# S4D with a gated unit: exponential as squares, angles without a reciprocal, low parts and skip weights on other engines

## The chip, the cores and the metric

The kernel runs on one core of a Trainium2 chip, as a single launch. The metric is device time in microseconds (us), the median of several runs. Engines are PE (TensorE; its weight load is PEld), DVE (VectorE), ACT (ScalarE), POOL (GpSimd) and SP (which only issues transfers). L705 is line 705 of the kernel before; in the kernel after most lines stand two to four further down (L442 there is L438 here).

## What is computed

`out = x + S4D(xn) + GLU(xn)` with `xn` the layer norm of x, for 2048 tokens, D = 448 channels, N = 256 states and F = 1792 hidden units in fp32. Of the reference this is the core:

```python
dt = exp(log_dt);  A = -exp(log_A_real) + 1j * A_imag;  C = (C_real + 1j * C_imag) * dt
K = 2 * einsum("dn,dnl->dl", C, exp(A * dt * l)).real      # l = 0 .. 2047
y = irfft(rfft(xn, 2L) * rfft(K, 2L))[:L] + xn * D_skip
glu = (sigmoid(xn @ w_gate) * (xn @ w_up)) @ w_down
```

So for every channel and state the kernel needs an exponential (the decay), the magnitude and angle of C, and from these the phases at all lags. The skip term is a weight at lag 0 of K: the kernel adds D_skip there.

## The kernel before

Two generators, `conv()` for the S4D branch and `glu()` for the gated unit, are run in turns (L1117 to L1127): the one with the smaller share of its planned work goes next. What they emit goes through a scheduler that fixes each engine's order of instructions. All products are done as fp32r matmuls with a split of each operand in a high and a low part (xh, xl; wh, wl; hh, hl; dh, dl), three products each.

`glu()` works on groups of up to three blocks of 128 hidden units and on halves of 512 tokens. For each block and half, `gate` issues 22 matmuls of 512 columns into two PSUM tiles gu (L705), a tanh th on ACT (L713), the product hf on DVE (L716), its high part hh on ACT (L721) and low part hl on DVE (L723). Then the down product po (L818, 448 columns, nine matmuls for a piece of 128 tokens in a group of three blocks, so 72 for the eight pieces) is added into acc by DVE (L823). The four PSUM slots of gu serve po, too. The weights of a block come in through one buffer (wraw); ACT casts the high part wh (L755), DVE subtracts for the low one wl (L759).

`conv()` starts with the norm and the transposes of x (L212; the parts xh, xl, xr at L221 to L225). Then comes the prep, in two halves of tiles of 112 x 512 (two groups of 112 channels, 256 states each), interleaved step by step:

- `exp()` (L303 to L318) computes the exponential of the decay logarithm: a rounding on ACT, the rest by a two-part log 2 on DVE, a polynomial of six steps on DVE (L316), an exponent built as an integer (L317), and the last product ex (L318). hdt, four multiples of dt, are made from its last columns on ACT (L354).
- Tanh and Exp of the decay times dt (L360 to L365) give what the powers need; their product pl goes through `turn` (L431): PE transposes (L438) into the PSUM tiles ko and kp, ACT copies (L440).
- The angle of C: the larger of the two absolute values, its reciprocal in four pieces of 128 columns (`pieces`, L320 to L322), the ratio of smaller to larger w, arctangent (L375), signs and offsets (L371 to L391), sine and cosine (L386, L387). L375 and L386 need different function tables.
- The phases U, V, T (L409 to L416) are split in a high part (a cast on ACT, L401) and a low part (a subtraction on POOL, L406); both go to DRAM over SP's queue.

Between the steps of the prep, `x_spec` (L283) sends the first transform of x through PE (L281) into the PSUM tiles tr, ko and kp, from where ACT copies it (L294 for tr, L296 for ko and kp) and stores it. ko, kp and tr have one buffer each; who writes them next waits for the copies.

`kgen` then makes K in 56 chunks: POOL multiplies up magnitudes me, mf for two chunks at a time (L504, L516), ACT squares a part (L529) and makes sines S (L544 to L547) of phases that PE spreads (tr, L538); DVE multiplies them to Et and Ft (L598 to L600; Ft has one buffer), and PE adds products of these in the PSUM tile ko (L612). After each fourth chunk (14 times, a bank) a small matmul (L622) adds the skip weights dm at lag 0, ACT copies ko to ks (L625), and `first_stage` (L562) takes ks to the first step of the transform. The spectra and the inverse follow (L900, L927).

Of the kernel before, what the change touches and what calls it, by code (L numbers as in the profile page):

```python
# [21 lines left out]
N = 256  # L22
# [4 lines left out]
TWO_PI = 2.0 * math.pi  # L27
MAGIC = 1.5 * 2.0**23
# [10 lines left out]
CP = D // 4  # L39
# [91 lines left out]
def s4d_glu_kernel(ctx, tc, io):  # L131
    nc = tc.nc
    hp = tc.high_priority
    v = nc.vector
# [16 lines left out]
    const = ctx.enter_context(tc.tile_pool(name="const", bufs=1, side="left"))  # L151
    ident = const.tile([128, 128], F32, name="ident")
# [16 lines left out]

    lim = const.tile([128, 2, 3], F32, name="lim")  # L170
# [132 lines left out]
    def exp(ex, ki, fr, pl):  # L303

        v.tensor_scalar(ex, ex, lim[:CP, 0, 1:2], lim[:CP, 0, 2:3], ALU.min, ALU.max)
        yield
        nc.scalar.activation(ki, ex, AF.Identity, scale=1.0 / math.log(2.0))
        yield
        ln2h = 0.693359375
        ln2l = math.log(2.0) - ln2h  # L310
        v.scalar_tensor_tensor(fr, ki, -ln2h, ex, ALU.mult, ALU.add)
        v.scalar_tensor_tensor(fr, ki, -ln2l, fr, ALU.mult, ALU.add)
        cs = [1.0 / math.factorial(i) for i in range(8)]
        nc.scalar.activation(pl, fr, AF.Identity, scale=cs[7])
        for i in range(6, 0, -1):
            v.scalar_tensor_tensor(pl, pl, cs[i], fr, ALU.add, ALU.mult)  # L316
        v.tensor_scalar(ki, ki, 127.0, 8388608.0, ALU.add, ALU.mult)  # L317
        v.scalar_tensor_tensor(ex, pl, 1.0, ki.bitcast(F32), ALU.add, ALU.mult)  # L318

    def pieces(t):  # L320
        for i in range(0, 2 * N, 128):
            v.reciprocal(t[:, i : i + 128], t[:, i : i + 128])  # L322

# [17 lines left out]
    def prep(pool, h, srcs):  # L341
# [3 lines left out]
        a3, b3, m3, w3, s3 = (new(n) for n in ("a3", "b3", "m3", "w3", "s3"))  # L345
# [6 lines left out]
        yield from exp(ex, ki, fr, pl)  # L352
# [14 lines left out]
        v.scalar_tensor_tensor(m3, a3, 1e-37, b3, ALU.max, ALU.max)  # L367
        pieces(m3)
        v.tensor_tensor(w3, a3, b3, ALU.min)
        v.tensor_tensor(w3, w3, m3, ALU.mult)  # L370
        v.tensor_tensor(s3, a3, b3, ALU.subtract)  # L371
        nc.scalar.activation(s3, s3, AF.Sign)
        nc.scalar.activation(cr, cr, AF.Sign)
        with tc.issue_after(exps[0].ins):
            nc.scalar.activation(w3, w3, AF.Arctan)  # L375
# [9 lines left out]
        v.scalar_tensor_tensor(w3, w3, -math.pi / 4, s3, ALU.add, ALU.mult)  # L385
# [3 lines left out]
        nc.scalar.activation(w3, w3, AF.Identity, bias=hpi[:CP])  # L389
        v.tensor_scalar(ci, ci, 0.0, -2.0 / TWO_PI, ALU.is_lt, ALU.mult)  # L390
        v.scalar_tensor_tensor(w3, ci, 1.0 / TWO_PI, w3, ALU.add, ALU.mult)  # L391
        yield
# [64 lines left out]
    def kgen(pk):  # L457
# [124 lines left out]
        for g in range(NCK // NCH):  # L582
            for c in range(NCH):
# [36 lines left out]
                if cn % 4 == 3:  # L620
                    ks = tl["ks"]
                    nc.tensor.matmul(  # L622
                        ko[:, :, 0], ident, dm[:, cn // 4], start=False, stop=True, skip_group_check=True
                    )
                    nc.scalar.copy(ks, ko)  # L625
                yield WK / 2
# [391 lines left out]
    def conv():  # L1018
        with tc.tile_pool(name="psk", bufs=1, space=PSUM) as ps_, tc.tile_pool(
# [9 lines left out]
            with tc.tile_pool(name="pst", bufs=1, side="right", reuse_waits="tile") as pst:  # L1029
# [125 lines left out]
```

## Time and profile before

| what | value |
|---|---|
| median of 3 runs | 723.75 us (722.47, 728.36, 723.75) |
| profiled execution | 724.73 us |
| its span, first to last instruction | 722.9 us |
| mean granted clock of PE | 0.980 of full speed |
| PE busy | 676.9 us, 94% of the span |
| DVE busy | 553.6 us, 77% |
| ACT busy | 428.6 us, 59% |
| POOL busy | 361.9 us, 50% |
| chain that ended last | 63% of it on PE, 11% DVE, 9% ACT |

A line of the timeline has the start, the duration, the engine and line, the operation, the written tile and the read ones, and in brackets the idle time ahead of it with what ended it. A line of waits has engine, tile and line that waited, what it waited for, the sum in us, the number of times and the longest. Successive instructions on an engine overlap by some tenths of a us, so what one costs is the distance from start to start where the engine is full. PE's granted clock is given as a share of full speed.

### The profile page before, as it was taken

What the parts mean: (1) busy time and instruction counts of PE and PEld (TensorE: products, weight loads), DVE (VectorE), ACT (ScalarE), POOL (GpSimd) and SP (SyncE); (2) the same over time, 40 slices, a digit from 0 to 9 for tenths busy, and PEclk for the clock granted to TensorE, in tenths of its full rate; (3) what the DMA queues carried; (4) which work ended last, traced back from release to release, by engine and by line L of the source; (5) the groups of instructions that cost most, each with busy time, mean ns of one, the idle gap of its engine ahead of it and who ended that gap; (6) DMA issues with size and microseconds to landing.
All of it is one profiled execution on the core that took longest, in us unless ns stands there. A gap on an engine that the chain in (4) does not pass through costs nothing.

```text
span 722.9 us, 19254 instructions
## 1 busy us (share of the span) xinstructions
PE 676.9 (94%) x7780; PEld 532.5 (74%) x7780; DVE 553.6 (77%) x760; ACT 428.6 (59%) x678; POOL 361.9 (50%) x423
## 2 busy tenths in 40 slices
PE   3898999999999898999999999998999999999995
PEld 2676887778877785666778877877877777776784
DVE  6899887689889899688488988978956555575543
ACT  3655966488688768795686786787642322313320
POOL 2101177656997966775365697586944002441001
PEclk9998999999999999899999999999999999999998
DMA  9948164464254444556942332332269999999845
GB/s 215 240 123 228 39 201 159 149 198 139 63 167 136 136 114 135 151 162 185 261 133 83 106 111 75 96 114 84 61 183 270 267 255 241 252 258 216 200 121 161
DMA packets 102985, 117.25 MB, mean 162 GB/s; under 512 B 13232, under 2 KB 90864, under 8 KB 102896
## 3 DMA queue, kind: packets, MB, share of 16 engines
q1 hardware_dynamic: 78736, 91.87, 46.0%
q10 hardware_dynamic: 21584, 18.24, 9.5%
q0 software_dynamic: 2576, 5.90, 3.0%
q8 instruction: 62, 1.02, 0.6%
q14 instruction: 27, 0.22, 0.1%
HBM read 72.13 MB, written 43.84 MB: 160 GB/s over the span
## 4 chain that ended last, share of the span: by engine, by line
PE 63%; DVE 11%; ACT 9%; DMA 6%; issue 4%; SPq 2%; POOL 2%; ACTq 1%; POOLq 0%; DVEq 0%
PE gu L705 27%; PE po L818 14%; PE sp L900 7%; PE ko L612 5%; PE pv L927 4%; PE tr L538 3%; DVE Ft L600 2%; DVE Et L599 2%; DVE Et L598 2%; ACT S L547 1%; ACT S L545 1%; ACT S L544 1%; SPq L640 1%; DVE pm L452 1%; DMA ph<-ph_d 1%
## 5 line engine op out<-in xcount | busy, mean ns | idle before, releaser
L516 POOL TENSOR_TENSOR me<-me,pm 128x32 f32<-128x32 f32 (+1 forms) x168 | 138.2, 823 | 104.4 <-DVE Et L599 87.9
L516 POOL TENSOR_TENSOR mf<-mf,pm 128x64 f32<-128x64 f32 (+1 forms) x112 | 121.1, 1081 | 4.7
L705 PE MATMUL gu<-xh,wh 128*128 128x512 f32 x336 | 100.8, 407 | 0.9 <-ACT xh L221 0.7
L705 PE MATMUL gu<-xh,wl 128*128 128x512 f32 x336 | 97.3, 397 | 0.0
L705 PE MATMUL gu<-xl,wh 128*128 128x512 f32 x336 | 97.3, 396 | 0.0
L598 DVE TENSOR_TENSOR Et<-me,S 128x1024 f32<-128x1024 f32 x56 | 82.8, 1479 | 11.9 <-ACT S L547 11.8
L818 PE MATMUL po<-dh,hh 128*128 128x448 f32 x224 | 85.5, 382 | 4.3 <-DVE hf L716 2.9
L599 DVE TENSOR_TENSOR Et<-me,S 128x1024 f32<-128x1024 f32 x56 | 78.1, 1394 | 13.3 <-ACT me L529 6.3
L818 PE MATMUL po<-dl,hh 128*128 128x448 f32 x224 | 83.5, 373 | 0.0
L600 DVE TENSOR_TENSOR Ft<-mf,S 128x1024 f32<-128x1024 f32 x56 | 78.7, 1405 | 5.6 <-ACT S L547 2.7
L544 ACT ACTIVATE S<-tr 128x1024 f32<-128x1024 f32 x56 | 57.8, 1032 | 41.9 <-PE tr L538 41.2
L818 PE MATMUL po<-dh,hl 128*128 128x448 f32 x224 | 82.5, 371 | 0.1
L705 PEld LDWEIGHTS gu<-xh,wh 128*128 128x128 f32 x336 | 61.8, 191 | 21.9 <-issue 4.4
L612 PEld LDWEIGHTS ko<-Et,Ft 128*32 128x32 f32 x3584 | 53.8, 110 | 32.4 <-DVE Ft L600 13.7
L612 PE MATMUL ko<-Et,Ft 128*32 128x64 f32 x3584 | 64.6, 221 | 11.9 <-DVE Ft L600 11.4
L705 PEld LDWEIGHTS gu<-xh,wl 128*128 128x128 f32 x336 | 64.3, 192 | 14.9 <-DVE hf L716 0.7
L705 PEld LDWEIGHTS gu<-xl,wh 128*128 128x128 f32 x336 | 64.3, 192 | 13.8
L721 ACT CAST hh<-hf 128x512 fp32r<-128x512 f32 x56 | 35.0, 625 | 65.9 <-DVE hf L716 60.1
L716 DVE SCALAR_TENSOR_TENSOR hf<-th,gu 128x512 f32<-128x512 f32 x56 | 38.2, 682 | 36.9 <-PE gu L705 31.7
L547 ACT ACTIVATE S<-S,hpi 128x1024 f32<-128x1024 f32 x56 | 65.6, 1171 | 1.3 <-issue 1.3
L823 DVE SCALAR_TENSOR_TENSOR acc<-po,acc 128x448 f32<-128x448 f32 x80 | 48.0, 616 | 23.5 <-PE po L818 23.5
L723 DVE TENSOR_TENSOR hl<-hf,hh 128x512 fp32r<-128x512 f32 x56 | 47.7, 851 | 18.2 <-ACT hh L721 18.2
(209 smaller groups left out, 1281.4 us busy)
## 6 DMA issues: line engine op xcount, KB each, us to landing
sk_d<-sk ACTq DMA_DIRECT2D x14, 512.0 KB
sx<-x_d SPq DMA_DIRECT2D x32, 224.0 KB
skl<-sk_d SPq DMA_DIRECT2D x16, 448.0 KB
vp<-v_d SPq DMA_DIRECT2D x16, 448.0 KB
v_d<-vt SPq DMA_DIRECT2D x62, 112.0 KB
ph<-ph_d SPq DMA_DIRECT2D x224, 24.0 KB
wt_d<-wh SPq DMA_DIRECT2D x9, 512.0 KB
wt_d<-wl SPq DMA_DIRECT2D x9, 512.0 KB
```

Of the source, the lines that this page charges most:

```text
L516: ins = nc.gpsimd.tensor_tensor(m[:, :, w + a : 2 * w : n], m[:, :, a:w:n], par(base + i).unsqueeze(2).to_broadcast([128, 4 * DC, w // n]) ...
L544: nc.scalar.activation(rows(cs), pv, AF.Abs)
L547: sins[:] = [nc.scalar.activation(cs, cs, AF.Sin, scale=-TWO_PI, bias=hpi)]
L598: v.tensor_tensor(Et[:, :, :, 32:64], two(me[:, :, 32:64]), S[:, 1::-1], ALU.mult)
L599: v.tensor_tensor(Et[:, :, :, 0:32], two(me[:, :, 0:32]), S[:, 1:3, :, ::-1], ALU.mult)
L600: fts[:] = [v.tensor_tensor(Ft, two(mf), S[:, 3:5], ALU.mult)]
L612: mm = nc.tensor.matmul(ko[32 * j : 32 * j + 32, sl], Ft[:, cc, DC * h + 4 * q + j], Et[:, cc, DC * h + 4 * q + j], start=(k == 0), stop=( ...
L705: glu_mm[:] = [nc.tensor.matmul(ps, a_, b_, start=(n == 0), stop=(n == len(mm) - 1))]
L723: v.tensor_tensor(hl, hf, hh, ALU.subtract)
L818: glu_mm[:] = [nc.tensor.matmul(po, a_[:, bs], w_, start=(n == 0), stop=(n == 3 * fc - 1))]
L823: v.scalar_tensor_tensor(acc[:, b], po, 0.5, acc[:, b], ALU.mult, ALU.add)
L900: mm = nc.tensor.matmul(to, tb[:kk, t, 64 * c : 64 * c + 64], rhs, start=True, stop=True, skip_group_check=True,)
```

## The change

- `exp()`: the polynomial of six steps becomes a product of three factors, with two squares: ACT makes Square(fr + a), Square(s fr + b) and adds a constant to the second; DVE makes (fr + r) fr, (pl + k) sq and their product. The exponent's integer is made by an Identity on ACT instead of L317. Per half DVE has four instructions less there, ACT three more.
- The angle: no reciprocal. The argument of the arctangent is (a - b) / (a + b); the inverse of the sum m starts from an integer operation on its bits (an Identity on ACT that reads and writes int32), and is refined by two steps in which DVE multiplies and ACT squares. Per half that takes the place of four reciprocals, a minimum and a product on DVE and of one Sign on ACT. The offsets of the angle are merged: ACT scales the sign of cr and makes the sign of ci, and DVE's comparison on ci (L390) and a product by s3 go.
- `low()`: the subtraction of the low phase parts goes from POOL to DVE (six instructions).
- The skip weights: the matmul at L622 goes; ACT copies ko to ks, then POOL adds dm into the column of lag 0 of ks.
- Seven constants are set in a tile bz by POOL at the start. The tile m3 becomes two columns wider and is used by `exp()` as well.

In the orders that the scheduler makes of it, these places are the ones that matter below. A name is a tile, with a number of its buffer; `out<-in`.

PE, at the end of the first group's po. In before both transposes of the first half stand behind the last po, here po_825, and ahead of the next gate, gu_849:

```order
L818 MATMUL po_825<-dh_421,hl_509 128x448
L818 MATMUL po_825<-dh_615,hh_667 128x448
L818 MATMUL po_825<-dl_618,hh_667 128x448
L818 MATMUL po_825<-dh_615,hl_668 128x448
L438 MATMUL ko_784<-ident_67,pl_384 128x112 x2
L438 MATMUL kp_788<-ident_67,pl_384 128x112 x2
L705 MATMUL gu_849<-xh_94,wh_836 128x512 x3
```

In after they stand after the sixth of the eight pieces, po_783, with po_818 and po_829 behind them:

```order
L820 MATMUL po_783<-dh_621,hh_673 128x448
L820 MATMUL po_783<-dl_624,hh_673 128x448
L820 MATMUL po_783<-dh_621,hl_674 128x448
L442 MATMUL ko_794<-ident_67,pl_392 128x112 x2
L442 MATMUL kp_798<-ident_67,pl_392 128x112 x2
L820 MATMUL po_818<-dh_265,hh_465 128x448
L820 MATMUL po_818<-dl_266,hh_465 128x448
L820 MATMUL po_818<-dh_265,hl_466 128x448
```

The transposes moved ahead by 18 matmuls.

ACT, at the last group of x_spec's copies (to x1ab), which free ko and kp. In before they stand ahead of the first hdt and of all Tanh and Exp:

```order
L713 ACTIVATE th_663<-gu_621 128x512
L294 COPY x1ab_376<-tr_671 128x896
L296 COPY x1ab_376<-ko_672 128x448
L300 DMA x1_d_59<-x1ab_376 64x2x448
L755 CAST wh_975<-wraw_976 128x1024
L296 COPY x1ab_376<-kp_673 128x448
L300 DMA x1_d_59<-x1ab_376 64x2x448
L354 ACTIVATE hdt_385<-ex_150 112x2 x4
```

In after the first hdt stands 55 rows ahead of the copy from ko, and the sines with their tables are ahead of the copies, too:

```order
L392 ACT_TABLE_LOAD
L392 ACTIVATE m3_389<-w3_387,qpi_75 112x512
L393 ACTIVATE s3_388<-w3_387,qpi_75 112x512
L414 ACTIVATE ki_402<-aim_159 112x512
L405 CAST p01_383<-aim_159 112x512
L297 COPY x1ab_384<-tr_677 128x896
L384 ACT_TABLE_LOAD
L384 ACTIVATE junk_81<-w3_399 112x1
L392 ACTIVATE m3_401<-w3_399,qpi_75 112x512
L393 ACTIVATE s3_400<-w3_399,qpi_75 112x512
L299 COPY x1ab_384<-ko_678 128x448
L299 COPY x1ab_384<-kp_679 128x448
```

Nearly all of the prep's work on ACT moved ahead of the last copies of x_spec.

DVE, ahead of a product hf of the first group (hf_609 in before):

```order
L322 RECIPROCAL m3_379<-m3_379 112x128 x2
L322 RECIPROCAL m3_391<-m3_391 112x128 x3
L759 TENSOR_TENSOR wl_844<-wraw_837,wh_836 128x1024
L322 RECIPROCAL m3_391<-m3_391 112x128
L316 SCALAR_TENSOR_TENSOR pl_384<-pl_384,fr_383 112x514
L316 SCALAR_TENSOR_TENSOR pl_396<-pl_396,fr_395 112x514
L260 SCALAR_TENSOR_TENSOR z_87<-z_87,ve_86 128x8
L716 SCALAR_TENSOR_TENSOR hf_609<-th_607,gu_595 128x512
```

The same product in after (hf_615):

```order
L761 TENSOR_TENSOR wl_848<-wraw_841,wh_840 128x1024
L373 SCALAR_TENSOR_TENSOR w3_387<-m3_389,w3_387 112x512
L372 TENSOR_TENSOR m3_401<-m3_401,w3_399 112x512
L373 SCALAR_TENSOR_TENSOR w3_399<-m3_401,w3_399 112x512
L387 SCALAR_TENSOR_TENSOR pl_404<-pl_404,ki_402 112x512
L718 SCALAR_TENSOR_TENSOR hf_615<-th_613,gu_601 128x512
```

The reciprocals and the last steps of the polynomial are gone from ahead of it, and products of the new angle stand there.

The diff, cut to its core:

```diff
+    bz = const.tile([128, 7], F32, name="bz")
...
-    def exp(ex, ki, fr, pl):
+    def exp(ex, ki, fr, pl, sq):
...
-        cs = [1.0 / math.factorial(i) for i in range(8)]
-        nc.scalar.activation(pl, fr, AF.Identity, scale=cs[7])
-        for i in range(6, 0, -1):
-            v.scalar_tensor_tensor(pl, pl, cs[i], fr, ALU.add, ALU.mult)
-        v.tensor_scalar(ki, ki, 127.0, 8388608.0, ALU.add, ALU.mult)
+        nc.scalar.activation(ki, ki, AF.Identity, scale=8388608.0, bias=bz[:CP, 3:4])
+        nc.scalar.activation(pl, fr, AF.Square, bias=bz[:CP, 0:1])
+        nc.scalar.activation(sq, fr, AF.Square, scale=EXP_S, bias=bz[:CP, 1:2])
+        nc.scalar.activation(sq, sq, AF.Identity, bias=bz[:CP, 2:3])
+        v.scalar_tensor_tensor(ex, fr, EXP_R, fr, ALU.add, ALU.mult)
+        v.scalar_tensor_tensor(pl, pl, EXP_K, sq, ALU.add, ALU.mult)
+        v.tensor_tensor(pl, pl, ex, ALU.mult)
         v.scalar_tensor_tensor(ex, pl, 1.0, ki.bitcast(F32), ALU.add, ALU.mult)
...
-        v.scalar_tensor_tensor(m3, a3, 1e-37, b3, ALU.max, ALU.max)
-        pieces(m3)
-        v.tensor_tensor(w3, a3, b3, ALU.min)
-        v.tensor_tensor(w3, w3, m3, ALU.mult)
+        v.scalar_tensor_tensor(m3, a3, 1e-37, b3, ALU.max, ALU.add)
+        nc.scalar.activation(w3.bitcast(I32), m3.bitcast(I32), AF.Identity, scale=-1.0, bias=bz[:CP, 4:5])
         v.tensor_tensor(s3, a3, b3, ALU.subtract)
-        nc.scalar.activation(s3, s3, AF.Sign)
+        v.tensor_tensor(m3, m3, w3, ALU.mult)
+        v.scalar_tensor_tensor(w3, m3, -2.0, w3, ALU.add, ALU.mult)
+        nc.scalar.activation(m3, m3, AF.Square, scale=-1.0, bias=one[:CP])
+        nc.scalar.activation(m3, m3, AF.Square, bias=bz[:CP, 5:6])
+        v.scalar_tensor_tensor(w3, m3, 0.75, w3, ALU.add, ALU.mult)
+        v.tensor_tensor(w3, w3, s3, ALU.mult)
         nc.scalar.activation(cr, cr, AF.Sign)
+        nc.scalar.activation(cr, cr, AF.Identity, scale=1.0 / TWO_PI)
+        nc.scalar.activation(ci, ci, AF.Sign, bias=bz[:CP, 6:7])
         with tc.issue_after(exps[0].ins):
             nc.scalar.activation(w3, w3, AF.Arctan)
...
-        v.scalar_tensor_tensor(w3, w3, -math.pi / 4, s3, ALU.add, ALU.mult)
         nc.scalar.activation(m3, w3, AF.Sin, bias=qpi[:CP])
         nc.scalar.activation(s3, w3, AF.Sin, scale=-1.0, bias=qpi[:CP])
         v.scalar_tensor_tensor(w3, w3, -math.pi / 4, cr, ALU.add, ALU.mult)
-        nc.scalar.activation(w3, w3, AF.Identity, bias=hpi[:CP])
-        v.tensor_scalar(ci, ci, 0.0, -2.0 / TWO_PI, ALU.is_lt, ALU.mult)
-        v.scalar_tensor_tensor(w3, ci, 1.0 / TWO_PI, w3, ALU.add, ALU.mult)
+        v.scalar_tensor_tensor(w3, w3, 0.25, ci, ALU.add, ALU.mult)
...
-            nc.gpsimd.tensor_tensor(lo, src, slots[f"P{i}"][:, h], ALU.subtract)
+            v.tensor_tensor(lo, src, slots[f"P{i}"][:, h], ALU.subtract)
...
-                    nc.tensor.matmul(
-                        ko[:, :, 0], ident, dm[:, cn // 4], start=False, stop=True, skip_group_check=True
-                    )
                     nc.scalar.copy(ks, ko)
+                    nc.gpsimd.tensor_tensor(ks[:, :, 0], ks[:, :, 0], dm[:, cn // 4], ALU.add)
...
+                for i, c in enumerate((EXP_A, EXP_B, EXP_C, 127.0 * 8388608.0, float(0x7EF30000), 0.5, 1e-37)):
+                    nc.gpsimd.memset(bz[:, i : i + 1], c)
```

More of the change, by code (lines that the diff above doesn't have):

```diff
@@ L27 @@
 TWO_PI = 2.0 * math.pi
+EXP_A, EXP_B, EXP_C = -0.8713653843588568, 0.07851670935535562, 0.011531916857233048
+EXP_K, EXP_S, EXP_R = 15.06237810040421, 0.03720672317048426, 3.5715240100230314
 MAGIC = 1.5 * 2.0**23
@@ L312, in exp @@
         v.scalar_tensor_tensor(fr, ki, -ln2l, fr, ALU.mult, ALU.add)
-        cs = [1.0 / math.factorial(i) for i in range(8)]
-        nc.scalar.activation(pl, fr, AF.Identity, scale=cs[7])
-        for i in range(6, 0, -1):
-            v.scalar_tensor_tensor(pl, pl, cs[i], fr, ALU.add, ALU.mult)
-        v.tensor_scalar(ki, ki, 127.0, 8388608.0, ALU.add, ALU.mult)
+        nc.scalar.activation(ki, ki, AF.Identity, scale=8388608.0, bias=bz[:CP, 3:4])
[5 more added lines that the diff above has]
+        v.tensor_tensor(pl, pl, ex, ALU.mult)
         v.scalar_tensor_tensor(ex, pl, 1.0, ki.bitcast(F32), ALU.add, ALU.mult)
-    def pieces(t):
-        for i in range(0, 2 * N, 128):
-            v.reciprocal(t[:, i : i + 128], t[:, i : i + 128])
     SF = [CP, 2 * N]
@@ L344, in prep @@
         new = lambda n, sh=SF, dt=F32: pool.tile(sh, dt, name=n, bufs=2)
-        a3, b3, m3, w3, s3 = (new(n) for n in ("a3", "b3", "m3", "w3", "s3"))
+        a3, b3, w3, s3 = (new(n) for n in ("a3", "b3", "w3", "s3"))
+        sq = new("m3", [CP, 2 * N + 2])
+        m3 = sq[:, : 2 * N]
         ki, fr, pl = new("ki", [CP, 2 * N + 2], I32), new("fr", [CP, 2 * N + 2]), new("pl", [CP, 2 * N + 2])
@@ L351, in prep @@
         nc.scalar.activation(b3, ci, AF.Abs, scale=lim[:CP, 1, 0:1])
-        yield from exp(ex, ki, fr, pl)
+        yield from exp(ex, ki, fr, pl, sq)
         for i, c in enumerate((0.5, -1.0, 1.0 / TWO_PI, 2.0)):
```

## Prediction

> **What bounds the kernel now.** I read first the page (busy times, chain), then the waits of TensorE, then the windows between 30 and 100 us, then the timelines of the engine that each wait names.
>
> The page's busy line of PE and its chain by engine, then, from the list of waits, what PE stood idle for (us in total, times, longest):
>
> ```profile
> PE 676.9 (94%) x7780; PEld 532.5 (74%) x7780; DVE 553.6 (77%) x760; ACT 428.6 (59%) x678; POOL 361.9 (50%) x423
> ...
> PE 63%; DVE 11%; ACT 9%; DMA 6%; issue 4%; SPq 2%; POOL 2%; ACTq 1%; POOLq 0%; DVEq 0%
> ```
>
> ```profile
> PE tr L212 <- DVE xn L270: 12.1, 1, 12.1
> PE ko L612 <- DVE Ft L600: 11.4, 10, 2.3
> PE po L818 <- DVE hf L716: 2.9, 1, 2.9
> PE gu L705 <- DVE xr L225: 2.7, 1, 2.7
> PE po L818 <- ACT hh L721: 1.4, 1, 1.4
> ```
>
> PE is the bound: 46 us of the 722.9 are not PE work, 12.1 of them before the first transpose, which the change does not touch. So an edit gains only if it shortens PE's work, closes one of these gaps, or spares the half clock that a gap brings. The prep of the convolution, where nearly all of the change lies, runs from 30 to 105 us. There the 2.9 us gap stands (PE's timeline, then the windows' row of these ten us: busy times, granted clock behind POOL's, DMA):
>
> ```profile
> 57.24 0.84 PE L705 MATMUL gu<-xl,wh 128*128 128x512 f32 x3
> ...
> 59.96 0.47 PE L818 MATMUL po<-dh,hl 128*128 128x448 f32 x1
> 63.35 0.74 PE L818 MATMUL po<-dh,hh 128*128 128x448 f32 x1 [2.91 <-DVE hf L716]
> ...
> 69.11 0.38 PE L818 MATMUL po<-dh,hl 128*128 128x448 f32 x1
> ```
>
> ```profile
> 60.00:70.00 10.00, 7.09 (x26) 6.08 (x22) 9.57 (x18) 4.84 (x12) 0.20 (x1) 0.66 0.74 208
> 70.00:80.00 10.00, 10.00 (x53) 9.14 (x51) 7.88 (x18) 9.95 (x22) 0.00 (x0) 1.00 0.39 98
> ```
>
> The gate's matmuls are done at 58, but the product that the next po needs comes off VectorE at 63.3. Behind the gap the granted clock is low: 0.66 over ten us is 6.8 us at a half, and 15 po take 5.76 us from 63.35 to 69.11, where 0.20 each at full clock (the step of the rows around 75.81 below, 18 po in 3.65) gives 3.05. The gap costs 2.9 and its half clock 2.7 more. VectorE was late for this reason:
>
> ```profile
> 55.35 4.19 DVE L322 RECIPROCAL m<-m 112x128 f32<-112x128 f32 x5
> ...
> 60.53 0.94 DVE L322 RECIPROCAL m<-m 112x128 f32<-112x128 f32 x1
> 61.39 1.23 DVE L316 SCALAR_TENSOR_TENSOR pl<-pl,fr 112x514 f32<-112x514 f32 x2
> ...
> 62.61 0.68 DVE L716 SCALAR_TENSOR_TENSOR hf<-th,gu 128x512 f32<-128x512 f32 x1
> ```
>
> Reciprocals (0.84 each) and polynomial steps (0.6) stood ahead of hf. ScalarE, in turn, is full from 70 to 80 (9.95 of 10 us) already.
>
> **The change part by part.** VectorE first. Per half the exponential loses six steps of 0.6 and one of 0.33 and gets three of 0.6; the angles lose four reciprocals of 0.84, one of 0.33 and get one of 0.6 more. That is 2.1 and 3.1 us, 10.4 over both halves; the six low parts put 6 x 0.6 = 3.6 back. hf is then no longer behind eight reciprocals (6.7 us), it comes at about 59, and the gap at 60 closes: -2.9 and -2.7.
>
> ScalarE gets twelve instructions more, six per half (7.3 us at 0.61), and a fourth table load (1.28) where there were three. Its durations, from its timeline (start to start, since they overlap):
>
> ```profile
> 64.34 0.90 ACT L294 COPY x1ab<-tr 128x896 f32<-128x896 f32 x1
> 65.13 0.55 ACT L296 COPY x1ab<-ko 128x448 f32<-128x448 f32 x1
> ...
> 67.23 1.05 ACT L755 CAST wh<-wraw 128x1024 fp32r<-128x1024 f32 x1 [1.55 <-DMA wraw<-in_B_w_up_dram]
> ...
> 70.58 0.60 ACT L721 CAST hh<-hf 128x512 fp32r<-128x512 f32 x1
> 71.09 0.51 ACT L360 ACTIVATE ki<-ex,hdt 112x256 f32<-112x256 f32 x1
> 71.51 0.47 ACT L354 ACTIVATE hdt<-ex 112x2 f32<-112x2 f32 x4
> 71.88 0.71 ACT L364 ACTIVATE pl<-fr,one 112x512 f32<-112x512 f32 x1
> 72.49 0.71 ACT L365 ACTIVATE ki<-ki,one 112x512 f32<-112x512 f32 x1
> 73.11 0.90 ACT L360 ACTIVATE fr<-ex,hdt 112x256 f32<-112x256 f32 x2
> 73.91 0.90 ACT L360 ACTIVATE ki<-ex,hdt 112x256 f32<-112x256 f32 x2
> ...
> 75.32 0.72 ACT L365 ACTIVATE ki<-ki,one 112x512 f32<-112x512 f32 x1
> 76.06 1.28 ACT L375 ACT_TABLE_LOAD   x1
> 77.35 1.15 ACT L375 ACTIVATE w<-w 112x512 f32<-112x512 f32 x2
> ```
>
> So a 112x512 activation is 0.61, a pair of halves 0.80, a cast 0.51, the wide copy 0.79, a narrow copy 0.52, a weight cast 0.95, four hdt 0.37, a load 1.28.
>
> In the new order the first transposes of the phases (turn, L438 before, L442 now) stand behind 54 po of the first group instead of 72, and they write the PSUM tiles ko and kp, which the last copies of x_spec (L299) must have left. So PE now waits there for ScalarE's copy of kp, its 57th instruction row from the first hdt on. That first hdt waits for VectorE's last step of the exponential, at about 46.9: in before hf starts at 46.96 behind eight such instructions (4.4 us), and eight of 0.6 take their place, with 0.6 of delay from an instruction placed ahead of xr. Up to the copy I count in ScalarE's new order 18 activations (11.0), six pairs (4.8), eleven casts (5.6), two weight casts (1.9), three wide and six narrow copies (2.4 and 3.1), three loads (3.8), eight hdt and the silu dummy (0.9): 33.5 us back to back. Some of these durations already hold waiting on a busy neighbour, so I take 32.9 and the end at 79.8. PE's side, by the row of the same po in before:
>
> ```profile
> 75.81 0.36 PE L818 MATMUL po<-dh,hl 128*128 128x448 f32 x1
> ...
> 79.46 0.35 PE L438 MATMUL ko<-ident,pl 112*128 112x112 f32 x2
> ```
>
> The 55th po stood at 75.81. Without gap and half clock it is 70.2; the delay at xr adds 0.6; ScalarE, now in arrears, makes PE wait at x_spec's third and fourth groups (about 0.9 and 1.4, tr must be copied first), at hh and hl of two blocks (0.9 and 0.7): 74.7. There it meets turn and stands still until 79.8, 5.1 us; the 55th po comes at 80.2, 4.3 us later than before. At 63.35 the half clock had begun 1.0 us ahead of the restart (6.8 us that end at 69.1), 1.9 us into the gap; the same here gives half clock from 76.6 to 83.4, of which 3.3 us hold work: 1.6 more. The transposes that stand earlier are missing later: -0.4. **In all +5.5 at 85 us**: the prep is lighter on VectorE and heavier on ScalarE, and PE waits for the latter.
>
> The gap of 1.4 at 112 us (with what stands around it 1.6) has hf late behind the powers on VectorE; these come earlier now, so -1.6 (bounds -1.6 and 0).
>
> The skip weights. PE's 14 pairs of small matmuls go. The profile's rows of one pair and its successor:
>
> ```profile
> 511.14 0.39 PE L622 MATMUL ko<-dm,ident 128*128 128x8 f32 x2
> 511.38 0.72 PE L538 MATMUL tr<-sel,ph 128*128 128x512 f32 x2
> ```
>
> They take 0.24 from start to start: 14 x 0.24 = -3.4, bounds 0 (if PE only waits instead) and -5.5 (their full 0.39). In their place POOL adds 128x8 numbers, and PE's first stage (L562) waits for that instead of for the copy. The rows of the first bank's copy, of the POOL work behind it, and of the nearest small POOL instruction:
>
> ```profile
> 165.20 0.58 ACT L625 COPY ks<-ko 128x512 f32<-128x512 f32 x1
> ```
>
> ```profile
> 172.36 3.99 POOL L516 TENSOR_TENSOR me<-me,pm 128x32 f32<-128x32 f32 x3 [6.17 <-DVE Et L599]
> ...
> 469.64 0.31 POOL L504 TENSOR_TENSOR mf<-GG,pm 128x64 f32<-128x64 f32 x1
> ```
>
> POOL is idle for 6.17 us there, the add takes 0.31 of them, and the copy is done 6.6 us ahead of POOL's next work. The add costs nothing as long as that cover stands (bounds 0 and 14 x 0.31 = 4.3; the first is nearer). The seven new memsets come on POOL ahead of 11.6 us, where it is idle: nothing, and 0.3 us at most behind its first DMA issues. The low parts go from POOL, where they lasted until 105.8, to VectorE: the rows of the phases there show what they cost VectorE from beside:
>
> ```profile
> 94.90 0.68 DVE L414 SCALAR_TENSOR_TENSOR w<-fr,w 112x512 f32<-112x512 f32 x1
> ...
> 97.74 1.80 DVE L414 SCALAR_TENSOR_TENSOR w<-fr,w 112x512 f32<-112x512 f32 x1
> ```
>
> The same instruction takes 1.1 more while POOL subtracts (it and VectorE slow each other in this row), some four times; 3.6 added against that is nothing, and the phases reach DRAM at about the same time. Their stores stay on SP's queue, ahead of weight loads that PE needs 25 us later.
>
> The chunks of the kernel generator (200 to 330 us, gaps of 11.4 in total behind Ft) are set by VectorE, which the change leaves alone there: 0, bounds -4 (a late PE waits less) and the +13 of the second rival.
>
> Sum: 724.7 + 5.5 - 1.6 - 3.4 = **725.2 us** for the profiled execution, whose 724.73 lie 0.98 over the median of the three runs; against that median **724.3**.
>
> A rule speaks against the change. The Trainium skill, page "ScalarE: Activation LUTs", section "What ACT_TABLE_LOAD costs", gives a switch of tables about 1.28 us of load and 1.38 us of draining. Here the load of 1.28 agrees; the draining is not there: the instruction ahead starts at 75.32 and lasts 0.72, the load starts at 76.06, the next instruction at 77.35. By the page three loads would make PE's stall 4.1 us longer by estimate.
>
> **The rivals.**
> First, ScalarE is never in arrears (faster): its stretch up to the copy takes 24 us rather than 33, because the instructions next to an unburdened VectorE are shorter than these rows, and PE finds ko and kp empty at 71. The sum is then -2.9 - 2.7 + 0.6 - 1.6 - 3.4 = -10.0: 714.7, or 713.7 against the median. For it: the gap at 60 truly goes. Against it: ScalarE was at 9.95 of 10 in before, with less work. It is faster by over 1% if the copy ends before some 73.5: then turn stalls nothing and the small waits shrink from 3.9 to under 2.8.
>
> Second, POOL's add makes the generator's chain longer (slower). POOL's next magnitudes now stand behind an add that waits for ScalarE's copy, which waits for PE's last ko. VectorE's Et waits for magnitudes:
>
> ```profile
> POOL me L516 <- DVE Et L599: 87.9, 21, 8.2
> ```
>
> The cover is 4.2 us on average (87.9 in 21), and PE comes 5.5 us later by the forecast. If VectorE does not follow PE's delay, each of 13 banks loses what exceeds the cover; 1 us per bank makes 13, with the forecast's +0.5 738.2, or 737.3 against the median. It decides from half a us per bank (7.2 / 13). Against it: copy and chunks hang together, and a PE delay moves Et too.
>
> Third, each table load brings a drain, so the stall at turn is 4.1 longer: 728.4 against the median. Against it are the rows above. That is what the page's rule would give.
>
> **How the numbers follow.** The forecast has 0.50 (its own range 720 to 729), the first rival 0.20, the second 0.22, the third 0.08. The range reaches from the first rival to near the second, 713.5 to 736.5; half of either is outside, 0.2 in all. A measurement of this kernel tells about 1% (7.2 us) from no change. The first rival is faster by more, but for its nearer part: 0.18; the second slower, with an edge of the forecast and the third: 0.25; within 1% is 0.57.
>
> **What would show it.** In the trace after: no wait of po for VectorE's hf at 60; ScalarE without idle time from 47 to 80; a wait of PE at turn (L442) for ScalarE's copy of L299, about 5 us, with half clock behind it; no wait at 112; no L622; POOL's add in idle time, and first stage (L562) without a wait. The prediction is wrong if PE has no gap at L442, if POOL's magnitudes start later behind VectorE's Et than before, or if the waits behind Ft differ by over 4 us from 11.4.

## The result: 0.9% slower, by one wait that was foreseen and one gain that did not come

The changed kernel takes 731.33 us (median of 8 runs, 728.81 to 734.38), the kernel before 724.54 us (8 runs, 721.67 to 729.26): a ratio of 1.0087, interval 1.0059 to 1.0116. The prediction had 724.3 (a difference from before that can't be told, within 1%) and a range of 713.5 to 736.5. Against its own sum of 725.2 for the profiled execution, the one profiled after took 728.81 (span 727.0). It is the fastest of the eight; the granted clock falls with the time, from 0.980 in this one to 0.972 in the slowest, so a typical run holds a little more half clock than this trace shows.

The profile after, busy times and chain:

```profile
PE 675.3 (93%) x7752; PEld 528.3 (73%) x7752; DVE 547.1 (75%) x750; ACT 437.3 (60%) x691; POOL 367.0 (50%) x438
...
PE 58%; DVE 13%; DMA 9%; ACT 9%; issue 3%; POOL 3%; SPq 2%; ACTq 1%; POOLq 0%; DVEq 0%
```

PE works 1.6 us less and the span is 4.1 us longer: 5.7 us more of idle PE. Its waits in the changed kernel (us in total, times, longest):

```profile
PE tr L215 <- DVE xn L273: 12.2, 1, 12.2
PE ko L616 <- DVE Ft L604: 9.4, 10, 3.4
PE ko L442 <- ACT x1ab L299: 5.6, 1, 5.6
...
PE gu L284 <- DVE hf L718: 2.8, 1, 2.8
PE po L820 <- DVE acc L825: 1.9, 1, 1.9
...
PE kp L566 <- POOL ks L627: 1.2, 1, 1.2
```

The wait of po for hf (2.9) and the one for hh (1.4) are gone. In their place stands the first turn (L442), which waits 5.6 us for the last copies of x_spec on ScalarE (L299). Two more waits of over 1.5 us are new, both in the chunks: 2.8 us of gu for hf at 290 us and 1.9 us of po for acc at 344 us. PE's timeline there, from the last po ahead of turn to the end of the half clock:

```profile
75.77 0.37 PE L820 MATMUL po<-dh,hl 128*128 128x448 f32 x1
81.75 0.64 PE L442 MATMUL ko<-ident,pl 112*128 112x112 f32 x2 [5.62 <-ACT x1ab L299]
...
82.50 0.72 PE L820 MATMUL po<-dh,hh 128*128 128x448 f32 x1
83.02 0.57 PE L820 MATMUL po<-dl,hh 128*128 128x448 f32 x1
...
87.75 0.37 PE L820 MATMUL po<-dh,hl 128*128 128x448 f32 x1
...
88.57 0.36 PE L442 MATMUL ko<-ident,pl 112*128 112x112 f32 x2
...
88.89 0.95 PE L707 MATMUL gu<-xh,wh 128*128 128x512 f32 x3
```

From start to start a po takes 0.37 us up to 87.5 and 0.20 behind. ScalarE's timeline at the ends of the stretch that was counted in the prediction, and the windows' row over most of it (span, PE, PEld, DVE, ACT, POOL busy, clock, DMA):

```profile
49.03 0.48 ACT L356 ACTIVATE hdt<-ex 112x2 f32<-112x2 f32 x4 [2.00 <-DVE z L262]
...
81.19 0.51 ACT L299 COPY x1ab<-ko 128x448 f32<-128x448 f32 x1
81.60 0.53 ACT L299 COPY x1ab<-kp 128x448 f32<-128x448 f32 x1
```

```profile
50.00:70.00 20.00, 19.32 (x95) 13.52 (x94) 17.59 (x32) 20.00 (x42) 1.35 (x2) 0.91 0.59 173
```

From the first hdt to the end of the copy ScalarE takes 33.1 us, and it is busy for all of 20.00 us between 50 and 70. In before VectorE was the full engine there (19.57 of 20.00 us); now it is ScalarE.

### The profile page after: what moved, and what is told of

Read it like the earlier page. It is cut to its first block, busy times and chain, and to the rows that moved or that the text cites. A ratio compares the mean times of both kernels' runs of the same rounds, so it can differ in the third digit from the quotient of the medians.

```text
span 727.0 us, 19188 instructions
## 1 busy us (share of the span) xinstructions
PE 675.3 (93%) x7752; PEld 528.3 (73%) x7752; DVE 547.1 (75%) x750; ACT 437.3 (60%) x691; POOL 367.0 (50%) x438
## 3 DMA queue, kind: packets, MB, share of 16 engines
q1 hardware_dynamic: 78736, 91.87, 46.2%
## 4 chain that ended last, share of the span: by engine, by line
PE 58%; DVE 13%; DMA 9%; ACT 9%; issue 3%; POOL 3%; SPq 2%; ACTq 1%; POOLq 0%; DVEq 0%
PE gu L707 27%; PE po L820 12%; PE sp L902 5%; PE ko L616 5%; PE pv L929 3%; PE tr L542 3%; DVE Ft L604 2%; DVE Et L603 2%; DVE Et L602 2%; DMA vp<-v_d 2%; POOL me L520 1%; DMA xe<-in_A_u_dram 1%; PE kp L566 1%; ACT S L549 1%; DMA tb<-in_c_tab_dram 1%
## 5 line engine op out<-in xcount | busy, mean ns | idle before, releaser
L520 POOL TENSOR_TENSOR me<-me,pm 128x32 f32<-128x32 f32 (+1 forms) x168 | 145.7, 867 | 79.4 <-DVE Et L603 65.0
L520 POOL TENSOR_TENSOR mf<-mf,pm 128x64 f32<-128x64 f32 (+1 forms) x112 | 116.7, 1042 | 6.1
L707 PE MATMUL gu<-xh,wh 128*128 128x512 f32 x336 | 99.0, 402 | 2.0 <-ACT xh L224 1.3
L602 DVE TENSOR_TENSOR Et<-me,S 128x1024 f32<-128x1024 f32 x56 | 84.8, 1515 | 12.1 <-ACT S L551 11.1
L603 DVE TENSOR_TENSOR Et<-me,S 128x1024 f32<-128x1024 f32 x56 | 78.4, 1400 | 10.8 <-ACT me L533 10.8
L715 ACT ACTIVATE th<-gu 128x512 f32<-128x512 f32 x56 | 33.8, 604 | 55.3 <-PE gu L707 54.7
```

The source lines that it names most:

```text
L520: ins = nc.gpsimd.tensor_tensor(m[:, :, w + a : 2 * w : n], m[:, :, a:w:n], par(base + i).unsqueeze(2).to_broadcast([128, 4 * DC, w // n]) ...
L602: v.tensor_tensor(Et[:, :, :, 32:64], two(me[:, :, 32:64]), S[:, 1::-1], ALU.mult)
L603: v.tensor_tensor(Et[:, :, :, 0:32], two(me[:, :, 0:32]), S[:, 1:3, :, ::-1], ALU.mult)
L707: glu_mm[:] = [nc.tensor.matmul(ps, a_, b_, start=(n == 0), stop=(n == len(mm) - 1))]
```

## The experiments

All ratios are to the kernel before, on the same chip, with 95% intervals. The theory: **ScalarE is in arrears in the prep, and PE pays at turn.** Its rival: the loss is in the generator's chunks, through POOL's add of the skip weights.

### 1. Arctangents behind x_spec's copies (e1_copyfirst)

```diff
-            nc.scalar.copy(x1s_[1][:, j], kk[j][:, :D])
+            xcp[:] = [nc.scalar.copy(x1s_[1][:, j], kk[j][:, :D])]
...
-        with tc.issue_after(exps[0].ins):
+        with tc.issue_after(exps[0].ins), tc.issue_after(xcp[0].ins):
             nc.scalar.activation(w3, w3, AF.Arctan)
...
```

> The changed kernel with one edit: the arctangents, and so the table loads and sines behind them, are issued on ScalarE after the last copy of x_spec. Theory (PE stands at turn because the copies that free ko and kp stand behind the prep's work on ScalarE): some 8.6 us of loads, arctangents and sines leave the place ahead of the copies, so these end at about 73 instead of 82; PE's wait at L442 falls from 5.6 us to under 1, the 6.8 us of half clock at 81 go (3.4 us), and the time is 7 to 9 us below the changed kernel's, about 722 to 724. Rival (the loss is in the chunks, by POOL's add in the magnitudes' chain): the wait at L442 goes but the time stays within 2 us of the changed kernel's 731, since the chunks set the end.

Measured: 730.39 us, ratio 1.0047 (1.0025 to 1.0068). The first wait went, as both expected, but by the middle values the time fell by less than half of what the theory had (the two intervals overlap): a wait of the same size stood at the second turn. ScalarE's timeline of this kernel, from x_spec's last copy to the first turn's copies (L444), then PE's wait:

```profile
74.75 0.55 ACT L299 COPY x1ab<-kp 128x448 f32<-128x448 f32 x1
...
75.31 1.28 ACT L382 ACT_TABLE_LOAD   x1
...
85.92 0.32 ACT L444 COPY W<-ko 128x224 f32<-128x224 f32 x1
```

```profile
PE ko L442 <- ACT W L444: 5.6, 1, 5.6
```

x_spec's copies end 7 us earlier (75.3 against 82.1), and the loads, arctangents and sines that gave way now stand ahead of the copy that frees ko for the second turn. ko has one buffer; whatever ScalarE does in between, one of its copies is late. That speaks for arrears, not for one bad place in the order.

### 2. That, and turn's copies on VectorE (e5_turn_dve)

```diff
-            nc.scalar.copy(
+            v.tensor_copy(
                 dst[:, g : g + NCK // 4].rearrange("p g k e -> p k g e"),
                 ps[:, :, :CP].rearrange("p k (g e) -> p k g e", e=DC),
             )
```

> The first experiment (arctangents behind the last copy of x_spec) and besides turn's copies out of ko and kp on VectorE instead of ScalarE. In the first experiment the wait at the first turn went, but the second turn waited 5.6 us for the first one's copy, which ScalarE made behind its arctangents and sines. Theory (ScalarE's arrears are the loss, and whatever PE asks of it there comes late): with the copies on VectorE neither turn waits over 1 us, the 6.8 us of half clock behind go, and the time falls 6 to 9 us below the changed kernel's 731, to 722 to 725. Rival (the loss is in the chunks and would come back there): the waits go, the time stays within 2 us of 731.

Measured: 724.71 us, ratio 1.0001 (0.9974 to 1.0029): the whole loss against before is gone, with all of the new arithmetic and POOL's add still in place. One part of the expectation failed: a wait of the second turn remains, now for VectorE, and the windows' row from 80 to 90 us has a clock of 0.83, 3.4 us at a half.

```profile
PE ko L442 <- DVE W L444: 2.4, 1, 2.4
```

```profile
80.00:90.00 10.00, 7.58 (x29) 5.82 (x28) 8.25 (x15) 7.38 (x12) 1.39 (x1) 0.83 0.25 83
```

### 3. The skip weights alone, and taken back (e2_dm_only, e4_dm_back, e10_turn_dve_dm_back)

The edits are the piece of the diff at L622 to L625 alone, put into before (e2), taken out of the changed kernel (e4), and taken out of the kernel of experiment 2 (e10).

> The kernel before with the skip weights alone moved: no matmul, an add on POOL behind the copy. Theory: the add lies in POOL's idle time, PE loses 14 pairs of small matmuls: 3.4 us faster than before, 721, and no wait of the first stage (L562) above 1 us. Rival (POOL's add holds up magnitudes and first stage): 3 to 13 us slower than before, with waits of the first stage for the add and later magnitudes.

Measured: 727.44 us, ratio 1.0006 (0.9982 to 1.0029).

> The changed kernel with the skip weights as a matmul again (all else as changed). Theory: 3.4 us slower than the changed kernel, about 734. Rival (POOL's add costs more than the matmul): faster than the changed kernel by 3 us or more, 728 or less.

Measured: 731.69 us, ratio 1.0068 (1.0039 to 1.0097), where the changed kernel has 1.0087 (1.0059 to 1.0116).

> The fifth experiment (arctangents behind x_spec's copies, turn's copies on VectorE) with the skip weights as a matmul again, so the chunks stand in the order of before. Theory (moving the skip weights neither gains nor loses, because PE waits in the chunks for what it saves): within 2 us of the fifth experiment, a ratio to before of 0.998 to 1.003. Rival (the add on POOL is a gain of 3.4 us as predicted): 3 us slower than the fifth, a ratio of 1.004 or more.

Measured: 726.57 us, ratio 1.0006 (0.9977 to 1.0035), where experiment 2 has 1.0001.

In three pairs the move makes no difference that can be told. Neither the 3.4 us of gain nor the loss of the rival is there. The pages of experiment 2 and of e10, which differ by this edit alone, in that order:

```profile
span 724.3 us, 19183 instructions
...
PE 675.1 (93%) x7752; PEld 528.4 (73%) x7752; DVE 553.5 (76%) x758; ACT 434.6 (60%) x683; POOL 368.6 (51%) x438
```

```profile
span 723.2 us, 19248 instructions
...
PE 677.0 (94%) x7780; PEld 532.3 (74%) x7780; DVE 544.0 (75%) x758; ACT 434.7 (60%) x683; POOL 349.2 (48%) x424
```

Without the matmuls PE works 1.9 us less and stands 3.0 us longer (724.3 - 675.1 = 49.2 against 723.2 - 677.0 = 46.2). In the kernel with the add alone (e2) PE's longest wait for Ft is 3.4 us where before has 2.3, and these rows of its list show what else is new or longer:

```profile
PE ko L612 <- DVE Ft L600: 9.6, 9, 3.4
...
PE gu L281 <- DVE hf L714: 2.8, 1, 2.8
...
PE po L816 <- DVE acc L821: 1.9, 1, 1.9
PE kp L562 <- POOL ks L623: 1.2, 1, 1.2
PE ko L612 <- DVE Et L598: 0.8, 1, 0.8
```

The largest new one is gu's wait for hf, 2.8 us at 287 us. It stands in the lists of all eight kernels with POOL's add (2.8 us in six of them, 3.3 in e11, 5.7 in e8) and in none of the six with the matmul (before, e3, e4, e9, e10, e12). So what PE saved by the matmuls it stood at other places. The removal made the scheduler set the chunks in another order, and the prep a little, too (in e2 the wait of po for hf at 64 us is 4.4 us where before has 2.9); which of these waits comes from PE being early and which from the order is not told apart. POOL's add itself shows only in the last bank, where kp waits 1.2 us for it and before waits 0.7 us for the copy.

### 4. The low parts alone, and taken back (e3_low_only, e11_low_back)

The edit is the one line in `low()`, put into before (e3) and taken out of the changed kernel (e11).

> The kernel before with the low phase parts alone moved from POOL to VectorE; every other instruction keeps its place. Theory: no difference, within 1 us of before: VectorE gets 3.6 us of work between 85 and 105 and loses as much slowing by POOL. Rival (the low parts delay hf, powers or acc on VectorE, and PE waits): 2 to 4 us slower, with a longer wait of po at 112 us.

Measured: 723.79 us, ratio 0.9965 (0.9937 to 0.9993): a little faster, its interval just clear of 1, which neither had. The list of PE's waits in this kernel has one of po left:

```profile
PE po L818 <- DVE hf L716: 2.9, 1, 2.9
```

The wait for hh at 112 us (1.4, a gap of 1.6 with its surroundings) is gone. So the low parts on VectorE are no cost, and close this gap. That VectorE reaches hf earlier because POOL no longer slows it, as in the prediction's two rows of L414, fits this and is argued, not shown.

> The changed kernel with the low parts on POOL again; nearly every other instruction keeps its place. Theory (the low parts on VectorE gain 2.2 us at 112 us): the wait of po for hh at 112 us is back, 1.5 us or more with what stands around it, and the time is 1 to 3 us above the changed kernel's, 732 to 734. Rival (in the changed kernel PE is late anyway, so the wait is covered): within 1 us of the changed kernel.

Measured: 735.07 us, ratio 1.0126 (1.0093 to 1.0159), where the changed kernel has 1.0087. The place in the theory is wrong: its only wait of po is one for acc (2.0 us), none stands at 112 us; that PE comes there late anyway, as the rival has it, fits and is argued. The intervals of the two kernels overlap, and the profiled execution is the slowest of the six (738.97 us). What is longer in this trace lies in the chunks and the spectra: from 320 to 335 us the granted clock is 0.66 (1.00 in the changed kernel), 5 us of work lost, and a wait for ScalarE's vt of 3.3 us stands in the spectra. Why, stays open.

### 5. Exponential or angles of before (e6_exp_back, e7_ang_back)

The edits put the removed lines of `exp()`, or of the angles with `pieces`, back into the changed kernel.

> The changed kernel with the exponential of before: six polynomial steps on VectorE per half, three instructions per half less on ScalarE (3.7 us); angles, low parts and skip weights as changed. Theory: ScalarE starts its stretch later (hdt waits for six steps) but has a shorter row of work ahead of the last copies, so the wait at turn is 2 to 4 us instead of 5.6, and the time 2 to 4 us below the changed kernel's, 727 to 729. Rival (VectorE is what binds there, and the exponential's six steps make hf late): a wait of po for hf of 2 to 3 us comes back and the time is no better than 731.

Measured: 737.46 us, ratio 1.0163 (1.0122 to 1.0204).

> The changed kernel with the angles of before: reciprocals on VectorE, three instructions per half and one table load less on ScalarE (5 us); exponential, low parts and skip weights as changed. The first turn then stands behind 70 po and the last copies 10 rows nearer to the first hdt. Theory: no wait at turn over 1 us; the reciprocals stand ahead of hf again, and a wait of 2 to 3 us for it comes back; the time is 4 to 7 us below the changed kernel's, 724 to 727. Rival (the exponential's squares are what makes ScalarE late): the wait at turn stays at 4 us or more and the time at 729 to 732.

Measured: 730.49 us, ratio 1.0061 (1.0033 to 1.0089).

Neither kernel has a wait of 1 us or more at turn: the copy from kp that turn needs ends at 76.7 us in e6 and at 72.3 in e7, where the changed kernel has 82.1. Yet neither is the faster kernel that the theory made of this. Both have the same new trouble elsewhere. The windows' rows from 200 to 350 us, in the chunks, of before, of the changed kernel, of e6 and of e7, in this order (columns as above):

```profile
200.00:350.00 150.00, 140.53 (x2023) 104.16 (x2021) 129.27 (x143) 116.83 (x180) 107.17 (x121) 0.95 0.53 156
```

```profile
200.00:350.00 150.00, 138.97 (x2078) 102.85 (x2077) 134.11 (x145) 117.77 (x182) 125.26 (x131) 0.97 0.51 148
```

```profile
200.00:350.00 150.00, 133.24 (x2001) 98.41 (x2000) 132.58 (x140) 117.13 (x181) 119.69 (x129) 0.97 0.47 140
```

```profile
200.00:350.00 150.00, 133.46 (x1984) 98.71 (x1983) 130.12 (x141) 114.78 (x177) 115.12 (x126) 0.94 0.48 143
```

PE is busy for 5.5 us less there in e6 and e7 than in the changed kernel, though nothing in the chunks was edited: the scheduler set them in another order, with 3.0 us of waits for Et where the changed kernel has 1.0. The prep has other orders, too: in e6 the last copies stand ahead of the sines' table load, in e7 turn stands behind 70 po. So in these two orders one half of the added work makes no wait at turn; that it takes both halves in the order of the changed kernel is not shown, and the times can't be used to price the halves.

### 6. x_spec's copies on VectorE (e8_x_dve)

```diff
-        nc.scalar.copy(x1s_[0], ps[:, :, :D])
+        v.tensor_copy(x1s_[0], ps[:, :, :D])
         for j in range(2):
-            nc.scalar.copy(x1s_[1][:, j], kk[j][:, :D])
+            v.tensor_copy(x1s_[1][:, j], kk[j][:, :D])
```

> The changed kernel with all copies of x_spec on VectorE instead of ScalarE: 7 us of work less in ScalarE's full stretch, and tr, ko and kp no longer wait for it. Theory: no wait at turn over 1 us, none at x_spec's third and fourth group, 6 to 10 us below the changed kernel's 731, so 721 to 725. Rival (VectorE becomes the late one): hf is late by 2 to 3 us at one or two places and the time stays above 727.

Measured: 734.44 us, ratio 1.0128 (1.0093 to 1.0163). The wait at turn is gone. The two longest new waits:

```profile
PE gu L284 <- DVE hf L718: 5.7, 1, 5.7
PE po L820 <- DVE acc L825: 4.5, 2, 4.2
```

Of the second row, 4.2 us lie at 80 us, in the prep: VectorE, now laden with the copies, reaches the addition to acc late, behind three copies of x_spec (73.8 to 76.6 us) and products of the prep. The first row stands at 291 us, in the chunks, where no copy of x_spec is; the changed kernel has 2.8 us there. So the rival is right that VectorE is late in its turn, at one place in the prep; the other place belongs to the order of the chunks.

### 7. Order alone, on VectorE (e9_recip_behind, e12_fr_behind)

If order decides, before can be made faster without new arithmetic. e9 is before with the low parts on VectorE and the reciprocals issued behind hl of the late product, where PE does not wait for what they delay:

```diff
-        pieces(m3)
+        with tc.issue_after(hls[-2].ins):
+            pieces(m3)
...
-            v.tensor_tensor(hl, hf, hh, ALU.subtract)
+            hls.append(v.tensor_tensor(hl, hf, hh, ALU.subtract))
...
```

> The kernel before with the low parts on VectorE, as in the third experiment, and one more edit: VectorE's reciprocals are issued behind the low part hl of the product that was late at 60 us, instead of ahead of that product; no arithmetic is changed. Theory (that gap is VectorE's order and nothing else, worth 2.9 us and 2.7 of half clock): po's wait for hf at 60 us goes and with it the half clock from 62.5 to 69.4, and the time falls by 4 to 6 us below the third experiment, to 718 to 720 where before is 724 to 726 (ratio 0.989 to 0.993). Rival (the reciprocals are late wherever they stand, and angles and turn wait for them): a wait of similar size appears at turn or for the next hf, and the ratio stays at 0.996 or above.

Measured: 721.1 us, ratio 0.9936 (0.9913 to 0.9960). It beats both kernels; no other run is below it. The wait for hf and the windows' row from 60 to 70 us of this kernel:

```profile
PE po L819 <- DVE hf L717: 0.8, 1, 0.8
```

```profile
60.00:70.00 10.00, 8.69 (x45) 5.94 (x46) 10.00 (x16) 8.36 (x24) 0.20 (x1) 1.00 0.75 211
```

PE is busy for 8.69 us where before had 7.09, at full clock where it had 0.66. The gain over e3's 0.9965 is 0.3% by the middle values, with intervals that overlap, short of the 4 to 6 us expected, and the ratio lies between the two expectations, near the theory's. In these ten us PE is still idle for 1.3, in small waits for copies of x_spec and, at 68.5 us, the 0.8 for hf.

> The ninth experiment (low parts on VectorE, reciprocals behind hl) and one more edit of order: the exponential's first two steps on VectorE, per half, are issued behind xr instead of ahead of it. Theory (whatever VectorE does ahead of a product that PE needs is paid by PE, with the half clock behind): PE's wait for xr at 32 to 35 us falls from 2.75 us to under 1 and the 3.4 us of half clock at 35.8 go, 3 to 4 us faster than the ninth: a ratio to before of 0.987 to 0.990. Rival (the prep is then late, and the next hf or turn waits for it): a wait of 2 us or more at hf or turn between 55 and 85 us, and a ratio of 0.993 or above.

The edit sets the first step of the exponential in `with tc.issue_after(xls[0].ins):`. Measured: 723.1 us, ratio 0.9970 (0.9946 to 0.9993): no better than e9, by the middle values worse. PE's waits in this kernel:

```profile
PE tr L281 <- ACT x1ab L294: 2.4, 1, 2.4
...
PE gu L707 <- DVE xr L225: 0.6, 2, 0.3
```

The wait for xr did fall, from 2.7 in before to 0.3 us, and one of 2.4 us for a copy of x_spec came up at 58 us with half clock behind (0.50 from 60 to 65 us). The gain at 33 us was given back 25 us later, at another place than the rival had named.

## Why the prediction was right or wrong

- **The gap at 60 goes (-2.9, -2.7).** The wait went: no wait of po for hf is left, and e9 shows by order alone that the reciprocals made it. The half clock went only in part. The windows' row from 60 to 64 us and PE's rows of x_spec's third group:

```profile
60.00:64.00 4.00, 4.00 (x12) 3.09 (x11) 3.89 (x5) 4.00 (x9) 1.14 (x1) 0.57 1.03 322
```

```profile
56.31 0.39 PE L707 MATMUL gu<-xh,wl 128*128 128x512 f32 x1
57.25 0.98 PE L284 MATMUL tr<-xn,wx 32*64 32x448 f32 x8 [0.54 <-ACT x1c L297]
58.28 0.97 PE L284 MATMUL ko<-xn,wx 32*64 32x448 f32 x4
59.33 0.97 PE L284 MATMUL kp<-xn,wx 32*64 32x448 f32 x4
60.22 1.20 PE L707 MATMUL gu<-xh,wl 128*128 128x512 f32 x2
```

Here tr, ko and kp are written one after another over 3 us, since ScalarE frees them one by one, and the gate's matmuls behind take 0.6 instead of 0.39: 3.4 us at a half, 1.7 of work lost. The prediction had foreseen waits at this place, not the clock. It does not add to the lag behind turn, since PE only reaches turn later and waits there for ScalarE all the same (next items).

- **ScalarE's row of work to the last copy is 32.9 us.** It is 33.1. In the changed kernel, e4 and e11, which have this row in common, turn starts again 32.7 us behind the first hdt each time (49.03 to 81.75, 48.31 to 81.02, 48.98 to 81.69), which fits that ScalarE alone sets that moment.
- **The first hdt starts at about 46.9.** This is the step that failed in the sum for the prep: it starts at 49.03. Two rows ahead of it:

```profile
46.76 0.69 DVE L323 SCALAR_TENSOR_TENSOR ex<-pl,ki 112x514 f32<-112x514 f32 x1
...
47.07 1.92 ACTq L303 DMA_DIRECT2D x_d<-x1ab  x2
```

VectorE's ex is done at 47.45, 0.5 late. This 0.5 is there from 19 us on (PE's first product with xr starts at 19.56 where before has 19.05), ahead of the prep. With the 0.6 that was put it makes the gate 1.1 late at xr (row below, 34.79 in before). The other 1.6 us go by while ScalarE issues two of x_spec's stores (ACTq, 47.07 to 48.99); the first hdt starts 0.04 behind that. In e1, e4, e5 and e11 it starts 0.04 to 0.05 us behind the end of the same issue, too (at 48.74, 48.31, 49.42 and 48.98). The profile names VectorE's z as what ended this idle time, but hdt does not read z. The prediction let hdt wait for VectorE alone; by these five traces it also stands behind ScalarE's own issues, though no run takes them away to test it.

```profile
35.93 0.50 PE L707 MATMUL gu<-xr,wh 128*128 128x512 f32 x1 [2.74 <-DVE xr L228]
```

- **PE stands 5.1 us at turn.** It is 5.6, and the copies waited for are the ones named. PE came there at 76.1 and not 74.7, and the copies ended at 82.1 and not 79.8: both ends were late, and that the difference agrees is in part luck.
- **The lag at 85 us is 5.5.** Too small. The first gate behind turn starts at 88.89; the row of the same matmul in before:

```profile
79.90 0.50 PE L705 MATMUL gu<-xh,wh 128*128 128x512 f32 x1
```

That is 9.0 later, 8.6 without the second turn's transposes (0.4), which before makes behind this place. The 3.1 us that are missing come from two terms. Turn starts again at 81.75 and not 79.8, by the late start above: 2.0. And the half clock behind turn lasts to 87.5, some 2.9 us of work lost where 1.6 were put: 1.3. The two make 3.3, 0.2 more than is missing.

- **The gap at 112 goes (-1.6).** It is gone. In before the low parts alone close it (e3); the prediction had the powers' place on VectorE as its reason and priced the low parts at nothing. But in the changed kernel with the low parts on POOL again (e11) no wait stands there either, so the earlier powers, or PE's lateness, are enough there; which, is not shown.
- **The skip weights (-3.4).** This is the other term that was mis-sized: three pairs of runs give 0. The lower bound stood in the prediction ("if PE only waits instead"), and was the case: PE works 1.9 us less and waits longer at other places (experiment 3). The cover was there, but the add takes 1.05 us in the median of 14, not 0.31.
- **The chunks (0).** From 8.6 at 89 us the lag falls to the 4.1 of the whole span; 1.6 of that belongs to the gap at 112. The other 3 us come back behind it, and no term of the sum has them. They are not fewer waits: less for Ft (9.4 in all where before had 11.4) is made up for by the new waits for hf and acc, and behind the rows of 88.89 and 79.90 PE is idle for 28.1 us in the changed kernel and for 27.5 in before. PE is busy for 5.5 us less there (610.0 against 615.5). Some 1.9 of these are the matmuls of the skip weights (experiment 3), and 1.7 a half clock in the chunks that the changed kernel does not have. The windows' rows from 320 to 330 us, before and after:

```profile
320.00:330.00 10.00, 9.78 (x92) 6.62 (x88) 8.12 (x9) 6.65 (x12) 4.60 (x4) 0.83 0.48 112
```

```profile
320.00:330.00 10.00, 8.41 (x145) 4.80 (x144) 9.50 (x12) 10.00 (x17) 9.38 (x12) 1.00 0.55 152
```

The rest was not told apart.

- **The rivals.** ScalarE never in arrears: false. POOL's add in the magnitudes' chain: not so, POOL still stands 65.0 us in 20 waits for Et ahead of the magnitudes (87.9 in 21 before), and the first stage waits once, for 1.2 us. Table loads with a drain: false here. The three loads lie in the stretch of 33.1 us, 0.2 from the sum without drains, and ScalarE's rows around the first of them, as around the two others, leave no room:

```profile
69.50 1.07 ACT L757 CAST wh<-wraw 128x1024 fp32r<-128x1024 f32 x1
...
70.59 1.28 ACT L382 ACT_TABLE_LOAD   x1
71.88 0.63 ACT L382 ACTIVATE w<-w 112x512 f32<-112x512 f32 x1
```

The 1.38 us of draining that the Trainium skill's page "ScalarE: Activation LUTs" (section "What ACT_TABLE_LOAD costs") adds to each load is in none of these rows; its 1.28 us of load is.

The sum that comes out: +8.6 where 5.5 was put, -1.6 as put, nothing as a term of its own for the skip weights where -3.4 was put, and -3 where 0 was put for the chunks, which is what is left of the span and no separate measurement: 728.7 against 728.81. The misses of 3.1 and 3.4 went one way and that of 3 the other; that the forecast of 725.2 came within 3.6 us is in part luck. The medians are further apart than the two profiled executions, 6.8 us against 4.1; the lower granted clock of the other runs goes along with it, and which gap starts the additional half clock in them is not known, as only the fastest was profiled.

## What to carry to other kernels

Work taken off a busy engine (here VectorE) gained nothing as long as it went to the engine that the bound one asks for something next: list the copies that free single-buffered PSUM tiles, count the rows that stand ahead of them in the new order, with the issues of transfers among them, and compare that sum with the bound engine's time of arrival. A gap or a half clock that only shortens such a wait costs nothing of its own, so add up along the engine that ends the wait. Removing instructions from the bound engine gained nothing here either, since it waited longer elsewhere. Where the order is made by a scheduler, an edit at one place can reorder a far one, so compare the far stretch's waits and busy time (here 200 to 350 us) before a time is put down to the edit. The fastest kernel of all (e9, 0.9936) has the old arithmetic, the low parts on VectorE and a changed order.

## What the runs showed of the hardware

The half clock did not need a long wait: 3 us of small matmuls of 32 rows (32x448), with no wait above 0.54 us in the rows, were followed by 3.4 us at half clock, where in before the wait of 2.91 us was followed by 6.8. GpSimd's add of 128x8 numbers took 0.2 us in its shortest and 1.05 in its median run, so its price is not set by its size. ScalarE's issue of two stores took 1.4 to 1.9 us in five traces, and its next instruction started 0.04 to 0.05 us behind the end of it; ScalarE is not counted as busy in this time.
